# Token halves sharing a PSUM bank, the first 128 tokens alone through the normalisation chain, and the state parts of block 0 last

## The chip, the cores and the metric

The kernel runs on one core of one Trainium2 chip. The metric is the device time of one execution in microseconds (us); the profile's span is about 1.8 us shorter than that time. Before the change the median was 182.52 us over four runs (182.48 to 182.59).

The engines are named as the profile names them: PE (TensorE matmuls), PEld (its weight loads), DVE (VectorE), ACT (ScalarE), POOL (GpSimd), SP (the queue that issues most DMA transfers). PE writes its results to PSUM, in banks that the kernel uses 512 columns at a time; an eviction is the copy of a result out of a bank by DVE or ACT. A transfer lands when its last data has arrived. A hole is a stretch in which PE stands still.

## The reference

A layer normalisation of `x` (2048 tokens, 512 channels) feeds two branches, a diagonal state-space model and a gated feed-forward network. Both are added to `x`:

```python
xn = layernorm(x)
# A: Bu = xn @ B_bar ; h_t = Lam_bar * h_(t-1) + Bu_t ; yA = 2*Re(h @ C^T) + xn*Dskip
# B: yB = (gelu(xn @ w_gate) * (xn @ w_up)) @ w_down        (F = 1376 hidden rows)
out = x + yA + yB
```

## The kernel before

The 2048 tokens are cut into four blocks of 512 tokens; a block has four tiles of 128 tokens. For each block PE does gate and up matmuls (GU: 11 row blocks "ft" of 128 hidden rows), state-input matmuls (BU) and down matmuls (DN). A small scheduler in the kernel orders the instructions of each engine from estimated durations; PE and SP keep program order.

Only block 0 is special. Its tokens must be loaded, normalised and transposed before PE has anything to do, and PE is given warm-up matmuls meanwhile. Its first three row blocks are therefore done in token pieces:

```python
def d_pe(n_list):                       # estimate of matmul time for the scheduler
    return sum(max(n / 2.4 + 2.5, 64.0 + n / 4.7) for n in n_list)

def LN(b, js=range(4), on_act=False):   # statistics, sqrt, reciprocal, scaling of tiles js
    for j in js:
        V(bn_stats ...); V(bn_aggr ...)
    POOL(... mean ...)
    ACT(... variance + eps ...); ACT(... Sqrt ...)      # on_act
    V(reciprocal ...)
    for j in js: V(... (x - mean) * r ...)              # "ln_n"

def GU(b, fts=None, halves=False):
    ...                                 # two banks for each row block: gate, up
    if halves:
        for ft in fts: banks[ft] = (next_bank(), next_bank())
        part(WG, WGc, 0, 0, 1)          # gate, tile 0, three row blocks: 12 matmuls, N=128
        part(WG, WGc, 0, 1, 2)          # gate, tile 1
        part(WU, WUc, 1, 0, 2)          # up, tiles 0 and 1 together: N=256
        TR0(2, "V"); TR0(3, "A")        # transposes of tiles 2, 3; evicted by DVE and by ACT
        part(WG, WGc, 0, 2, 3); part(WG, WGc, 0, 3, 4); part(WU, WUc, 1, 2, 4)
    for ft in fts:
        ...                             # gelu on ACT, copy of up on ACT, product on DVE (512 columns)

# [cut] DN(b): for each tile j: seed, 11 hidden matmuls, 8 state matmuls, add, store

PE(fwarm, ...)                          # 11 warm-up matmuls, N=512
LN(0, [0, 1], True)
TR0(0, "V"); TR0(1, "A"); fill(4); params()
LN(0, [2, 3], True)
load_B()
GU(0, [0, 1, 2], halves=True)
tables_dve()
GU(0, [3, 4])
# [cut] tables, BU(0), CHAIN(0), ..., BU(1), ..., DN(0), ...
```

The loads go to SP in this order: tiles 0 to 3 of x (128 KB each), the first gate chunk (three row blocks, 384 KB), the first up chunk (384 KB), the second gate and the second up chunk (four row blocks, 512 KB each), then block 1's x and the transposing loads of B.

## Time and profile before

| | before |
|---|---|
| median time | 182.52 us |
| span | 180.8 us |
| PE, DVE, ACT busy | 97%, 86%, 51% |
| first gate matmul starts | 6.84 us |
| first state-input matmul of block 0 starts | 16.93 us |
| last matmul ends | 177.75 us |

From the page of the kernel before: busy time of each engine (share of the span, instructions).

```profile
span 180.8 us, 2356 instructions
...
PE 175.2 (97%) x848; PEld 82.8 (46%) x864; DVE 155.8 (86%) x264; ACT 92.0 (51%) x158; POOL 7.5 (4%) x19
```

The same kernel by windows: the head (first gate matmul to first state-input matmul) and the rest up to the last matmul. The columns are the length, each engine's busy time with its instructions, the granted clock, the DMA share and GB/s.

```profile
6.80:16.93 10.13, 9.36 (x97) 7.07 (x97) 9.45 (x29) 7.36 (x14) 2.34 (x3) 1.00 1.15 265
16.93:177.75 160.82, 160.02 (x730) 73.45 (x743) 141.61 (x222) 82.44 (x140) 3.88 (x6) 1.00 0.22 51
```

The second window holds 744 matmuls of 512 columns by the program (some records are missing in the trace). 160.82 us for 744 is 216 ns each. PE is busy through the window, so nothing in it is to be won from waits. What the change can touch is the head. All that PE waited for, by the view of waits (us in total, times, longest):

```profile
PE PS L790 <- DVE arena L508: 1.0, 1, 1.0
PE PS L717 <- DVE arena L637: 0.7, 1, 0.7
```

The head in order of time, PE (start us, duration, line, shapes, count; in brackets the idle time before and what ended it). L790 is the warm-up, L629 the tile transposes, L717 gate and up, L654 state input:

```profile
0.99 4.88 PE L790 MATMUL PS<-arena 128*128 128x512 bf16 x11 [0.99 <-DVE arena L508]
5.80 0.72 PE L629 MATMUL PS<-arena 128*128 128x128 bf16 x8
...
6.84 2.81 PE L717 MATMUL PS<-arena 128*128 128x128 bf16 x36
9.49 0.61 PE L629 MATMUL PS<-arena 128*128 128x128 bf16 x8
10.82 6.28 PE L717 MATMUL PS<-arena 128*128 128x128 bf16 x51 [0.72 <-DVE arena L637]
16.93 7.07 PE L654 MATMUL PS<-arena 128*128 128x512 bf16 x32
```

How to read this: the last number before "x" is the shape of the first matmul of the row only. The bracketed idle time is counted from the modelled end of the matmul before, which includes its drain; from start to start a hole is some 0.16 us longer. The hole at 10.1 to 10.8 us is where PE waits until tiles 2 and 3 have been normalised and evicted.

ACT in the same stretch: tile 3's eviction stands ahead of the load of gelu's table.

```profile
10.13 0.60 ACT L635 ACTIVATE arena<-PS 128x512 bf16<-128x512 bf16 x1 [2.06 <-PE PS L629]
10.75 1.28 ACT L745 ACT_TABLE_LOAD   x1
```

### The profile page before, as it was taken

The numbers are of one execution on the slowest core, as the hardware profiler recorded it, in microseconds if no ns is written. First come the engines' busy times: TensorE is split into PE (matmuls) and PEld (weight loads), VectorE is DVE, ScalarE is ACT, GpSimd is POOL, SyncE is SP. The second block draws the span as 40 slices with busy tenths as digits, with TensorE's granted clock in tenths as the row PEclk, the third lists the DMA queues.
The fourth block names the chain that finished last, engine by engine and source line by source line (L and its number), as shares of the span: only waits on it lengthen the run. The fifth ranks groups of instructions, "written<-read, shape, count | busy, mean of one in ns | idle before, by whom it ended". The sixth has DMA issues, their size and how long they took to land.

```text
span 180.8 us, 2356 instructions
## 1 busy us (share of the span) xinstructions
PE 175.2 (97%) x848; PEld 82.8 (46%) x864; DVE 155.8 (86%) x264; ACT 92.0 (51%) x158; POOL 7.5 (4%) x19
## 2 busy tenths in 40 slices
PE   7989999999999999999999999999999999999993
PEld 2674444444444444444444444444444444444441
DVE  4899679999999996999999999999989999982111
ACT  3378999776767997002667793000667700800000
POOL 2220202000000002000000000000000000000000
PEclk9999999999999999999999999999999999999999
DMA  5999914999000000001610000000000000021100
GB/s 128 305 325 165 313 31 103 244 320 189 14 0 0 4 0 0 29 29 60 90 30 0 0 2 0 33 29 29 29 0 0 4 0 0 0 87 35 54 31 29
DMA packets 24068, 12.38 MB, mean 68 GB/s; under 512 B 15385, under 2 KB 24057, under 8 KB 24057
## 3 DMA queue, kind: packets, MB, share of 16 engines
q1 hardware_dynamic: 24032, 12.23, 28.2%
q8 instruction: 7, 0.11, 0.2%
q14 instruction: 5, 0.03, 0.1%
q10 hardware_dynamic: 24, 0.00, 0.0%
HBM read 6.46 MB, written 2.10 MB: 47 GB/s over the span
## 4 chain that ended last, share of the span: by engine, by line
PE 95%; DVE 2%; issue 1%; ACT 0%; DVEq 0%
PE PS L717 41%; PE PS L773 36%; PE PS L654 15%; PE PS L790 3%; DVE arena L637 0%; DVE arena L608 0%; DVE arena L778 0%; DVE arena L595 0%; PE PS L629 0%; ACT arena L599 0%; ACT arena L600 0%; DVE arena L539 0%; DVE arena L596 0%; DVE arena L538 0%; DVE arena L553 0%
## 5 line engine op out<-in xcount | busy, mean ns | idle before, releaser
L717 PE MATMUL PS<-arena 128*128 128x512 bf16 (+3 forms) x393 | 76.7, 353 | 1.1 <-DVE arena L637 0.7
L773 PE MATMUL PS<-arena 128*128 128x512 bf16 (+1 forms) x296 | 65.6, 379 | 0.4
L717 PEld LDWEIGHTS PS<-arena 128*128 128x128 bf16 (+1 forms) x400 | 37.8, 100 | 38.9 <-DVE arena L637 0.9
L745 ACT ACTIVATE arena<-PS 128x512 bf16<-128x512 f32 (+1 forms) x44 | 26.3, 599 | 49.1 <-PE PS L717 37.1
L773 PEld LDWEIGHTS PS<-arena 128*128 128x128 bf16 (+1 forms) x304 | 29.7, 98 | 36.0
L687 DVE TENSOR_TENSOR_SCAN arena<-arena 128x512 bf16<-128x512 f32 x32 | 38.6, 1251 | 0.0
L748 ACT ACTIVATE arena<-PS 128x512 bf16<-128x512 f32 (+1 forms) x44 | 26.3, 600 | 6.7 <-PE PS L717 6.6
L654 PE MATMUL PS<-arena 128*128 128x512 bf16 x127 | 28.2, 379 | 0.1
L778 DVE TENSOR_TENSOR arena<-PS,arena 128x512 bf16<-128x512 f32 x16 | 10.8, 684 | 15.5 <-PE PS L773 15.5
L654 PEld LDWEIGHTS PS<-arena 128*128 128x128 bf16 x128 | 12.5, 98 | 15.0
L658 ACT ACTIVATE arena<-PS 128x512 bf16<-128x512 f32 x32 | 17.8, 596 | 2.1 <-PE PS L654 2.1
L750 DVE TENSOR_TENSOR arena<-arena 128x512 bf16<-128x512 bf16 (+1 forms) x44 | 17.4, 415 | 0.8 <-ACT arena L748 0.8
L595 DVE BATCH_NORM_STATS2 arena<-arena 128x6 f32<-128x512 bf16 x16 | 10.2, 680 | 3.5 <-DMA arena<-in_A_x_dram 3.5
L760 ACT ACTIVATE PS<-arena 128x512 f32<-128x512 bf16 x16 | 9.4, 603 | 0.7
L674 DVE TENSOR_TENSOR arena<-arena 128x4096 bf16<-128x4096 bf16 (+1 forms) x5 | 9.3, 1859 | 0.0
L676 DVE TENSOR_TENSOR arena<-arena 128x4096 bf16<-128x4096 bf16 (+1 forms) x5 | 9.3, 1858 | 0.0
L699 DVE TENSOR_TENSOR arena<-arena 128x4096 bf16<-128x4096 bf16 x4 | 9.2, 2288 | 0.1
L700 DVE TENSOR_TENSOR arena<-arena 128x4096 bf16<-128x4096 bf16 x4 | 9.1, 2284 | 0.0
L608 DVE TENSOR_SCALAR arena<-arena 128x512 bf16<-128x512 bf16 x16 | 5.6, 409 | 0.3
L615 DVE TENSOR_TENSOR arena<-arena 128x512 bf16<-128x512 bf16 x16 | 5.8, 416 | 0.0
L790 PE MATMUL PS<-arena 128*128 128x512 bf16 x11 | 4.9, 632 | 1.0 <-DVE arena L508 1.0
L571 DVE SCALAR_TENSOR_TENSOR arena<-arena 128x512 bf16<-128x512 bf16 x8 | 5.6, 747 | 0.0
(75 smaller groups left out, 66.1 us busy)
## 6 DMA issues: line engine op xcount, KB each, us to landing
out_dram<-arena SPq DMA_DIRECT2D x16, 128.0 KB, 1.7
arena<-in_A_x_dram SPq DMA_DIRECT2D x3, 512.0 KB, 7.6
arena<-in_B_w_down_dram SPq DMA_DIRECT2D x1, 1280.0 KB, 8.2
arena<-in_A_x_dram SPq DMA_DIRECT2D x4, 128.0 KB, 2.2
arena<-in_B_w_gate_dram SPq DMA_DIRECT2D x1, 512.0 KB, 5.8
arena<-in_B_w_up_dram SPq DMA_DIRECT2D x1, 512.0 KB, 6.7
arena<-in_B_w_gate_dram SPq DMA_DIRECT2D x1, 480.0 KB, 4.6
arena<-in_B_w_up_dram SPq DMA_DIRECT2D x1, 480.0 KB, 6.0
```

Source lines behind the costliest of these rows:

```text
L595: V(lambda e, tt=tt: e.bn_stats(ST[tt].ap, X[tt].ap), d_dve_1x(512), [X[tt]], [ST[tt]], "bnst")
L654: ins_ = e.matmul(PS[bank][:, :], BBT[c][dk].ap[:, 128 * s:128 * (s + 1)], XNT[b].ap[:, dk, :], start=(dk == 0), stop=(dk == KD - 1))
L658: ACT(lambda e, bank=bank, k3=k3, s=s, c=c: e.activation(SSc[k3][s][c].ap, PS[bank][:, :], ACTF.Copy), d_act(512), [BANK[bank]], [SSc[k3][ ...
L687: V(lambda e, g=g, rb=rb, init=init: e.tensor_tensor_scan(g.ap, rb, g.ap, init, ALU.mult, ALU.add), d_dve_scan(512), [g, PA[RRr]] + ([CARc ...
L717: ins_ = e.matmul(PS[bank][0:m, c0:c1], W.ap[:, dk, 128 * ft:128 * ft + m], XNT[b].ap[:, dk, c0:c1], start=(dk == 0), stop=(dk == KD - 1))
L745: GATE["last_gelu"] = ACT(lambda e, bg=bg, kk=kk, m=m: e.activation(GG[kk].ap[0:m, :], PS[bg][0:m, :], ACTF.Gelu_apprx_tanh), d_act(512), ...
L748: ACT(lambda e, bu=bu, kk=kk, m=m: e.activation(UPB[kk].ap[0:m, :], PS[bu][0:m, :], ACTF.Copy), d_act(512), [BANK[bu]], [UPB[kk]], "evU")
L750: V(lambda e, kk=kk, m=m, ft=ft, k2=k2: e.tensor_tensor(HTt[k2][ft].ap[0:m, :], GG[kk].ap[0:m, :], UPB[kk].ap[0:m, :], ALU.mult), d_dve_tt ...
L760: ACT(lambda e, bank=bank, tt=tt: e.activation(PS[bank][:, :], X[tt].ap, ACTF.Copy), d_act(512), [X[tt]], [BANK[bank]], "seed")
L773: ins_ = e.matmul(o_, l_, r_, start=False, stop=(n == len(mms) - 1), skip_group_check=True)
L778: V(lambda e, bank=bank, ko=ko, tt=tt: e.tensor_tensor(OUTB[ko].ap, PS[bank][:, :], XD[tt].ap, ALU.add), d_dve_1x(512), [BANK[bank], XD[tt ...
L790: ins_ = e.matmul(PS[wb][:, :].rearrange("p (a b) -> p a b", a=4), WRM.ap, wrm4, start=True, stop=True)
```

## The change

The intent: get the first tile to PE sooner by not making it wait for the second tile's statistics, and let a row block's gate and up results of half the tokens (256 columns each) share one 512-column bank, so that five row blocks can be worked on in halves. Block 0's down part first takes all hidden matmuls and then the state matmuls, to give block 0's states more time. The scheduler's estimates of matmul time and of the delay between matmuls are corrected.

```diff
+LAT = lambda d, op: SYNC_LAT if d.kind == "dma" or d.eng != op.eng else (0.0 if d.eng == "tensor" else SELF_LAT)
     # [cut] LAT used in the scheduler's two passes in place of SELF_LAT / SYNC_LAT
 def d_pe(n_list):
-    return sum(max(n / 2.4 + 2.5, 64.0 + n / 4.7) for n in n_list)
+    return sum(n / 2.4 + 2.5 for n in n_list)
 # [cut] LN takes "after", added to bn_stats
+        def GU_first(fts, early, single):
+            banks = [{ft: next_bank() for ft in fts} for h in range(2)]
+            def mm(ft, u, j0, j1):      # gate (u=0) in columns 0-255 of the bank, up (u=1) in 256-511
+                ...
+            def evac(ft, h, ...):       # gelu, copy and product of 256 columns
+                ...
+            for u in range(2):
+                for ft in early:
+                    mm(ft, u, 0, 1)                     # tile 0: gate, then up
+                    if single and u == 0 and ft == 1:
+                        TR0(1, "A")
+            for ft in early:
+                for u in range(2):
+                    mm(ft, u, 1, 2)                     # tile 1
+                evac(ft, 0)
+            late = [ft for ft in fts if ft not in early]
+            mm(late[0], 0, 0, 2)
+            TR0(2, "V")
+            TR0(3, "A")
+            for ft in late[1:]:
+                mm(ft, 0, 0, 2)
+            for ft in late:
+                mm(ft, 1, 0, 2)
+                evac(ft, 0)
+            for ft in fts:
+                for u in range(2):
+                    mm(ft, u, 2, 4)                     # second token half
+                evac(ft, 1)
 # [cut] GU loses its halves; DN is split into seed, hidden, states, store
+            if split:
+                for j in range(4):
+                    seed(j); hidden(j)
+                for j in range(4):
+                    states(j); store(j)
-        LN(0, [0, 1], True)
+        LN(0, [0], True)
         TR0(0, "V")
-        TR0(1, "A")
         fill(4)
         params()
-        LN(0, [2, 3], True)
+        LN(0, [1], True, [GATE["bnag"]])
+        LN(0, [2, 3], True, [GATE["evT"]])
         load_B()
-        GU(0, [0, 1, 2], halves=True)
+        GU_first(range(5), range(3), True)
         tables_dve()
-        GU(0, [3, 4])
 # [cut]
-        DN(0)
+        DN(0, True)
```

Gate and up in one bank are safe here because their accumulation groups follow one another and are never open together. The Trainium skill ("PSUM — Partial Sum Buffer", "The four PSUM rules") says that a group's first matmul clears the accumulation bits of the whole bank, and that two open groups cannot both do that.

More of the change, by code (lines that the diff above doesn't have):

```diff
@@ L203, in _backward @@
             for d in op.deps:
-                late[d.id] = min(late[d.id], begin[op.id] - (SELF_LAT if d.eng == op.eng and d.kind == "eng" else SYNC_LAT))
+                late[d.id] = min(late[d.id], begin[op.id] - LAT(d, op))
                 left[d.id] -= 1
@@ L224, in rdy_time @@
         def rdy_time(op):
-            return max([d.finish + (SELF_LAT if d.eng == op.eng and d.kind == "eng" else SYNC_LAT) for d in op.deps], default=0.0)
+            return max([d.finish + LAT(d, op) for d in op.deps], default=0.0)
         while nleft:
@@ L543, in build @@
         W16p = [A.sub(A.alloc("W16v", [4, 4], F32, at=W16.lo), "W16_%d" % i, i) for i in range(4)]
-        GATE = {"before_gelu": []}
+        GATE = {"before_gelu": [], "nh": 0}
         sinT, sinP, cosT, cosP = (SC16.ap[:, 4 * i:4 * i + 4] for i in range(4))
@@ L587, in tables_act, with LN @@
             return ACT(lambda e: e.activation(SINT.ap, F1.ap, ACTF.Sin, scale=-SIN_SCALE), d_act(2048), [F1], [SINT], "sint", after=[t])
-        def LN(b, js=range(4), on_act=False):
+        def LN(b, js=range(4), on_act=False, after=()):
             j0, j1 = js[0], js[-1] + 1
@@ L594, in LN @@
                 tt = 4 * b + j
-                V(lambda e, tt=tt: e.bn_stats(ST[tt].ap, X[tt].ap), d_dve_1x(512), [X[tt]], [ST[tt]], "bnst")
-                V(lambda e, tt=tt, j=j: e.bn_aggr(MVt[b][j].ap, ST[tt].ap), D_TINY, [ST[tt]], [MVt[b][j]], "bnag")
+                V(lambda e, tt=tt: e.bn_stats(ST[tt].ap, X[tt].ap), d_dve_1x(512), [X[tt]], [ST[tt]], "bnst", after)
+                GATE["bnag"] = V(lambda e, tt=tt, j=j: e.bn_aggr(MVt[b][j].ap, ST[tt].ap), D_TINY, [ST[tt]], [MVt[b][j]], "bnag")
             POOL(lambda e: e.tensor_copy(mn.ap, mv.ap[:, :, 0]), 200, [mv], [mn], "mn")
@@ L704, in CHAIN, with f, evac @@
               d_dve_tt2x(2048), [TA, TB], [SSc[k3][s][1] for s in range(KP)], "post_im")
-        def GU(b, fts=None, halves=False):
+        def GU_first(fts, early, single):
+            banks = [{ft: next_bank() for ft in fts} for h in range(2)]
+            def mm(ft, u, j0, j1):
+                W, Wc = ((WG, WGc), (WU, WUc))[u]
+                h, q0 = j0 // 2, 256 * u + 128 * (j0 % 2)
+                bank = banks[h][ft]
+                def f(e):
+                    ins_ = None
+                    for dk in range(KD):
+                        ins_ = e.matmul(PS[bank][:, q0:q0 + 128 * (j1 - j0)], W.ap[:, dk, 128 * ft:128 * (ft + 1)],
+                                        XNT[0].ap[:, dk, 128 * j0:128 * j1], start=(dk == 0), stop=(dk == KD - 1))
+                    return ins_
+                PE(f, d_pe([128 * (j1 - j0)] * 4), [Wc[wchunk(ft)]] + XT0[j0:j1], [BANK[bank]], "GU0")
+            def evac(ft, h):
+                bank, c0 = banks[h][ft], 256 * h
+                GATE["nh"] = kk = (GATE["nh"] + 1) % 3
+                GATE["last_gelu"] = ACT(lambda e: e.activation(GG[kk].ap[:, 0:256], PS[bank][:, 0:256], ACTF.Gelu_apprx_tanh),
+                                        d_act(256), [BANK[bank]], [GG[kk]], "gelu")
+                ACT(lambda e: e.activation(UPB[kk].ap[:, 0:256], PS[bank][:, 256:512], ACTF.Copy),
+                    d_act(256), [BANK[bank]], [UPB[kk]], "evU")
+                V(lambda e: e.tensor_tensor(HTt[0][ft].ap[:, c0:c0 + 256], GG[kk].ap[:, 0:256], UPB[kk].ap[:, 0:256], ALU.mult),
+                  d_dve_tt2x(256), [GG[kk], UPB[kk]], [HTt[0][ft]], "hmul")
+            for u in range(2):
[20 more added lines that the diff above has]
+                evac(ft, 1)
@@ L707, in GU @@
+        def GU(b, fts=None):
             k2 = b % 2
@@ L720, in mm @@
                 PE(f, d_pe([c1 - c0] * 4), [Wc[wchunk(ft)]] + rd, [BANK[bank]], "GU%d" % b)
-            if halves:
-                for ft in fts:
-                    banks[ft] = (next_bank(), next_bank())
-                def part(W, Wc, i, j0, j1):
-                    for ft in fts:
-                        mm(ft, W, Wc, banks[ft][i], 128 * j0, 128 * j1, XT0[j0:j1])
-                part(WG, WGc, 0, 0, 1)
-                part(WG, WGc, 0, 1, 2)
-                part(WU, WUc, 1, 0, 2)
-                TR0(2, "V")
-                TR0(3, "A")
-                part(WG, WGc, 0, 2, 3)
-                part(WG, WGc, 0, 3, 4)
-                part(WU, WUc, 1, 2, 4)
             for ft in fts:
                 m = FROWS[ft]
-                if not halves:
-                    banks[ft] = (next_bank(), next_bank())
+                banks[ft] = (next_bank(), next_bank())
                 bg, bu = banks[ft]
                 kk = (KF * b + ft) % 3
-                if not halves:
-                    for (W, Wc, bank) in zip((WG, WU), (WGc, WUc), banks[ft]):
-                        mm(ft, W, Wc, bank, 0, 512, XTr(b))
+                for (W, Wc, bank) in zip((WG, WU), (WGc, WUc), banks[ft]):
+                    mm(ft, W, Wc, bank, 0, 512, XTr(b))
                 GATE["last_gelu"] = ACT(lambda e, bg=bg, kk=kk, m=m: e.activation(
@@ L752, in GU, with DN @@
                   d_dve_tt2x(512), [GG[kk], UPB[kk]], [HTt[k2][ft]], "hmul")
-        def DN(b):
+        def DN(b, split=False):
             k2, k3 = b % 2, b % 3
-            for j in range(4):
-                tt = 4 * b + j
-                bank = next_bank()
-                ko = tt % 4
-                ACT(lambda e, bank=bank, tt=tt: e.activation(PS[bank][:, :], X[tt].ap, ACTF.Copy),
-                    d_act(512), [X[tt]], [BANK[bank]], "seed")
-                def f(e, bank=bank, j=j, k2=k2, k3=k3, b=b):
-                    mms = []
-                    for ft in range(KF):
-                        m = FROWS[ft]
-                        mms.append((PS[bank][:, :], HTt[k2][ft].ap[0:m, 128 * j:128 * (j + 1)], WD.ap[0:m, ft, :]))
-                    for s in range(KP):
-                        for c in range(2):
-                            mms.append((PS[bank][:, :], SSc[k3][s][c].ap[:, 128 * j:128 * (j + 1)], CT[c][s].ap))
-                    ins_ = None
-                    for n, (o_, l_, r_) in enumerate(mms):
-                        ins_ = e.matmul(o_, l_, r_, start=False, stop=(n == len(mms) - 1), skip_group_check=True)
-                    return ins_
-                rds = [HTt[k2][ft] for ft in range(KF)] + WDc
-                rds += [SSs[k3][s] for s in range(KP)] + [CT[c][s] for c in range(2) for s in range(KP)]
-                PE(f, d_pe([512] * (KF + 8)), rds + [BANK[bank]], [BANK[bank]], "DN%d" % b)
-                V(lambda e, bank=bank, ko=ko, tt=tt: e.tensor_tensor(OUTB[ko].ap, PS[bank][:, :], XD[tt].ap, ALU.add),
@@ new lines, in DN, with seed, mms, f @@
+            banks = [next_bank() for _ in range(4)]
+            def seed(j):
+                tt, bank = 4 * b + j, banks[j]
+                ACT(lambda e: e.activation(PS[bank][:, :], X[tt].ap, ACTF.Copy), d_act(512), [X[tt]], [BANK[bank]], "seed")
+            def mms(j, ops, last, rds):
+                bank = banks[j]
+                def f(e):
+                    ins_ = None
+                    for n, (l_, r_) in enumerate(ops):
+                        ins_ = e.matmul(PS[bank][:, :], l_[:, 128 * j:128 * (j + 1)], r_, start=False,
+                                        stop=last and n == len(ops) - 1, skip_group_check=True)
+                    return ins_
+                PE(f, d_pe([512] * len(ops)), rds + [BANK[bank]], [BANK[bank]], "DN%d" % b)
@@ new lines, in hidden, with states, store @@
+            def hidden(j):
+                ops = [(HTt[k2][ft].ap[0:FROWS[ft], :], WD.ap[0:FROWS[ft], ft, :]) for ft in range(KF)]
+                mms(j, ops, False, [HTt[k2][ft] for ft in range(KF)] + WDc)
+            def states(j):
+                ops = [(SSc[k3][s][c].ap, CT[c][s].ap) for s in range(KP) for c in range(2)]
+                mms(j, ops, True, [SSs[k3][s] for s in range(KP)] + [CT[c][s] for c in range(2) for s in range(KP)])
+            def store(j):
+                tt, bank = 4 * b + j, banks[j]
+                ko = tt % 4
+                V(lambda e: e.tensor_tensor(OUTB[ko].ap, PS[bank][:, :], XD[tt].ap, ALU.add),
@@ L779, in DN @@
                   d_dve_1x(512), [BANK[bank], XD[tt]], [OUTB[ko]], "evO")
-                S.dma(lambda e, tt=tt, ko=ko: e.dma_start(out[0, 128 * tt:128 * (tt + 1), :], OUTB[ko].ap),
+                S.dma(lambda e: e.dma_start(out[0, 128 * tt:128 * (tt + 1), :], OUTB[ko].ap),
                       128 * 1024, reads=[OUTB[ko]], is_output=True, tag="st_out")
+            if split:
[3 more added lines that the diff above has]
+                    states(j); store(j)
+            else:
+                for j in range(4):
+                    seed(j); hidden(j); states(j); store(j)
```

## The prediction

> **What bounds the kernel now.** TensorE. The page shows PE busy 97% of 180.8 us; the chain of waits is 95% PE. From 16.93 us, where the timeline shows block 0's first state-input matmul, to the last matmul's end at 177.75, there are 744 matmuls of 512 columns at 216 ns: 160.7 us, the whole stretch. Nothing to win there: PE's waits are 1.0 us at the start and 0.7 at 10.8. The change can pay only before 16.93.
>
> **The head before (timeline).** Eleven warm-up matmuls hold the in-order PE from 0.99 to 5.87. Tile 0's ln_n is ready at 5.7, its transposes run at 5.80, its DVE eviction 6.27-6.69, the first gate matmul at 6.84. Then come 48 matmuls of 128 columns, 24 of 256 and 16 of 512, with one hole of 0.72 us before 10.82. Spacing read there: about 56, 109 and 216 ns, as the Trainium skill's "TensorE: Matmul & The Clock Gate", section "Back-to-back issue gap", gives for isolated warm matmuls (N/2.4+2.5); its 81 ns for N=128 is not seen here.
>
> **What the change does.**
> - Tile 0's bn_stats no longer waits for tile 1's (0.69 us), so ln_n ends at about 5.0. But the warm-up is unchanged and blocks PE to about 5.7, and the first weight chunk lands at 2.65+4.0 = 6.65. First gate matmul at about 6.68: only 0.15 us earlier.
> - PE work in fts 0-4: 48x56 + 56x109 = 8.8 us, against 8.76: equal.
> - ACT: 20 evictions of 256 columns (estimate 0.39 us each, 0.27 apart, from 0.60 and 0.48 at 512) for 10 of 512: 0.6 us more, off the chain.
> - PE reaches the second token half (needs tiles 2 and 3) at about 12.05. Tile 3's eviction now stands on ACT behind the 1.28 us gelu table load (possible only after the last sqrt, about 9.4) and four half evictions; before, it stood ahead. Estimate: load ends 10.7, eviction 11.8-12.4. Tile 2's stands on DVE behind an hmul that waits for those evictions: ends about 12.1. PE waits about 0.4 us. The skill's "ScalarE: Activation LUTs", "What ACT_TABLE_LOAD costs", gives 1283 ns, as this trace does; its further drain of about 1380 ns is not seen here.
> - The second half: 40x109 = 4.4 us, ending at 16.86 against 16.93.
> - Block 0's state parts last: its states are ready at 60.1, its down matmuls start at 67.17, so nothing waited. Worth 0.
>
> **Predicted time.** 0.1 to 0.3 us gained: 182.3 us, range 181.5 to 183.2 (8 in 10). Faster by over 2%: 0.01; within 2%: 0.98; slower by over 2%: 0.01.
>
> **What would show it.** First gate matmul at 6.6-6.75. A PE wait of 0.2-0.8 us at about 12, ended by the eviction of tile 2 or 3, in place of the 0.72 us hole. First state-input matmul within 0.7 us of 16.9. From there 160.7 us without a PE wait. DVE busy up by about 0.7 us.
>
> **What would make it wrong.** Weight chunks (landing about 7.73, 9.5, 10.9) are needed within 0.3 us of landing; a late one stalls PE. If tiles 2 and 3 are evicted before 12.05, PE runs unbroken and the gain is 0.7 us. If DVE's order drags tile 1 (its reciprocal now stands behind tile 0's eviction), stalls at 7.2 and 8.4 could add up to 0.5 us of loss. A changed order on DVE or ACT could open a wait in the long stretch, where the slack is 5 to 7 us.

## The result, and the profile after

The median after the change is 182.37 us over four runs (181.93 to 182.48), against 182.52 us. A ratio here is the mean time of one kernel's fast runs over that of the other's in the same rounds, so it is not quite the ratio of the medians. This one is 0.9987, with a 95% interval of 0.9970 to 1.0004: no difference clear of noise. In a later set of five rounds the same kernel gave 0.9982 (0.9970 to 0.9994), a gain of about 0.3 us. The profiled run after the change, at 182.48 us, is the slowest of its four.

The page of the changed kernel:

```profile
span 180.7 us, 2411 instructions
...
PE 174.4 (97%) x865; PEld 84.2 (47%) x880; DVE 156.7 (87%) x270; ACT 93.9 (52%) x170; POOL 9.7 (5%) x20
```

Its windows, the head and the rest:

```profile
6.60:16.85 10.25, 9.65 (x116) 8.85 (x117) 8.54 (x30) 8.39 (x23) 1.26 (x2) 1.00 1.12 269
16.85:177.67 160.82, 160.02 (x731) 73.43 (x743) 144.16 (x229) 83.06 (x142) 6.99 (x7) 1.00 0.21 52
```

The long stretch is 160.82 us again. The last matmul ends at 177.67 and not at 177.75, so the profiled run shows 0.08 us of gain, all of it in the head. PE's waits:

```profile
PE PS L839 <- DVE arena L509: 1.0, 1, 1.0
PE PS L718 <- DVE arena L609: 0.7, 1, 0.7
PE PS L718 <- DMA arena<-in_B_w_up_dram: 0.6, 1, 0.6
PE PS L630 <- DVE arena L609: 0.2, 1, 0.2
```

The head in order of time, PE (L839 warm-up, L630 transposes, L718 gate and up of block 0's first five row blocks, L655 state input; the record of the first state-input matmul is missing, its weight load ran at 16.74, and the second started at 17.06, so one spacing of 0.216 us earlier puts its start at 16.85):

```profile
0.99 4.03 PE L839 MATMUL PS<-arena 128*128 128x512 bf16 x11 [0.99 <-DVE arena L509]
5.19 0.40 PE L630 MATMUL PS<-arena 128*128 128x128 bf16 x4 [0.16 <-DVE arena L609]
...
6.63 0.62 PE L718 MATMUL PS<-arena 128*128 128x128 bf16 x8 [0.71 <-DVE arena L609]
7.08 0.39 PE L630 MATMUL PS<-arena 128*128 128x128 bf16 x4
7.31 0.39 PE L718 MATMUL PS<-arena 128*128 128x128 bf16 x4
8.27 2.62 PE L718 MATMUL PS<-arena 128*128 128x128 bf16 x40 [0.57 <-DMA arena<-in_B_w_up_dram]
10.72 0.61 PE L630 MATMUL PS<-arena 128*128 128x128 bf16 x8
11.17 5.84 PE L718 MATMUL PS<-arena 128*128 128x256 bf16 x52
```

The hole has moved. It is no longer at 10.1 us, but at 7.5 us: PE has done tile 0's gate matmuls and now wants the first up chunk, which before was wanted only after 24 gate matmuls. The chunk was issued at 3.13 us and landed 5.1 us later, at 8.22 us. From the list of DMA issues (KB each, us from issue to landing):

```profile
arena<-in_B_w_gate_dram SPq DMA_DIRECT2D x1, 384.0 KB, 3.9
arena<-in_B_w_up_dram SPq DMA_DIRECT2D x1, 384.0 KB, 5.1
```

The first gate matmul, at 6.63, follows a landing too: the first gate chunk was issued at 2.66 and landed at 6.56, while tile 0's eviction had ended at 6.04 us. The view of waits puts that wait down to DVE; the weight-load row before the same matmul names the gate chunk:

```profile
6.62 0.45 PEld L718 LDWEIGHTS PS<-arena 128*128 128x128 bf16 x8 [0.80 <-DMA arena<-in_B_w_gate_dram]
```

ACT in the same stretch (L601 is the last square root, L726 and L728 are half evictions, the first of four shown, L636 is tile 3's eviction):

```profile
8.41 0.20 ACT L601 ACTIVATE arena<-arena 128x2 bf16<-128x2 bf16 x1
8.63 1.28 ACT L726 ACT_TABLE_LOAD   x1
...
9.93 0.38 ACT L726 ACTIVATE arena<-PS 128x256 bf16<-128x256 f32 x1
...
11.37 0.60 ACT L636 ACTIVATE arena<-PS 128x512 bf16<-128x512 bf16 x1 [0.23 <-PE PS L630]
```

The load and four half evictions do stand ahead of tile 3's eviction, as predicted, but in this run PE is late anyway and nothing comes of it.

### The profile page after: what moved, and what is told of

Same layout as the page of the kernel before. It is cut to its first block, busy times and chain, and to the rows that moved or that the text cites. A ratio compares the mean times of both kernels' runs of the same rounds, so it can differ in the third digit from the quotient of the medians.

```text
span 180.7 us, 2411 instructions
## 1 busy us (share of the span) xinstructions
PE 174.4 (97%) x865; PEld 84.2 (47%) x880; DVE 156.7 (87%) x270; ACT 93.9 (52%) x170; POOL 9.7 (5%) x20
## 3 DMA queue, kind: packets, MB, share of 16 engines
HBM read 6.46 MB, written 2.10 MB: 47 GB/s over the span
## 4 chain that ended last, share of the span: by engine, by line
PE 93%; DMA 3%; SPq 1%; issue 1%; DVE 0%; DVEq 0%
PE PS L767 37%; PE PS L802 36%; PE PS L655 15%; PE PS L718 5%; DMA arena<-in_B_w_up_dram 3%; SPq L465 1%; DVE arena L818 0%; PE PS L630 0%; SPq L461 0%; DVEq L331 0%
## 5 line engine op out<-in xcount | busy, mean ns | idle before, releaser
L767 PE MATMUL PS<-arena 128*128 128x512 bf16 (+1 forms) x308 | 67.8, 379 | 0.2
L802 PE MATMUL PS<-arena 128*128 128x512 bf16 (+1 forms) x297 | 65.8, 379 | 0.4
L767 PEld LDWEIGHTS PS<-arena 128*128 128x128 bf16 (+1 forms) x312 | 31.4, 100 | 36.1
L779 ACT ACTIVATE arena<-PS 128x512 bf16<-128x512 f32 (+1 forms) x39 | 23.5, 603 | 46.2 <-PE PS L767 36.8
L802 PEld LDWEIGHTS PS<-arena 128*128 128x128 bf16 (+1 forms) x304 | 29.7, 98 | 36.0
L655 PE MATMUL PS<-arena 128*128 128x512 bf16 x124 | 27.7, 379 | 0.2
L782 ACT ACTIVATE arena<-PS 128x512 bf16<-128x512 f32 (+1 forms) x39 | 23.5, 602 | 7.2 <-PE PS L767 7.1
L655 PEld LDWEIGHTS PS<-arena 128*128 128x128 bf16 x128 | 12.5, 98 | 14.8
L784 DVE TENSOR_TENSOR arena<-arena 128x512 bf16<-128x512 bf16 (+1 forms) x39 | 15.5, 414 | 3.6 <-ACT arena L782 3.3
L596 DVE BATCH_NORM_STATS2 arena<-arena 128x6 f32<-128x512 bf16 x16 | 10.3, 682 | 1.4 <-DMA arena<-in_A_x_dram 1.3
L718 PE MATMUL PS<-arena 128*128 128x256 bf16 (+1 forms) x104 | 9.5, 248 | 1.3 <-DVE arena L609 0.7
L718 PEld LDWEIGHTS PS<-arena 128*128 128x128 bf16 x104 | 8.1, 98 | 2.1 <-DMA arena<-in_B_w_gate_dram 0.8
```

The costliest lines, as they stand in the source:

```text
L596: V(lambda e, tt=tt: e.bn_stats(ST[tt].ap, X[tt].ap), d_dve_1x(512), [X[tt]], [ST[tt]], "bnst", after)
L655: ins_ = e.matmul(PS[bank][:, :], BBT[c][dk].ap[:, 128 * s:128 * (s + 1)], XNT[b].ap[:, dk, :], start=(dk == 0), stop=(dk == KD - 1))
L718: ins_ = e.matmul(PS[bank][:, q0:q0 + 128 * (j1 - j0)], W.ap[:, dk, 128 * ft:128 * (ft + 1)], XNT[0].ap[:, dk, 128 * j0:128 * j1], start=( ...
L767: ins_ = e.matmul(PS[bank][0:m, c0:c1], W.ap[:, dk, 128 * ft:128 * ft + m], XNT[b].ap[:, dk, c0:c1], start=(dk == 0), stop=(dk == KD - 1))
L779: GATE["last_gelu"] = ACT(lambda e, bg=bg, kk=kk, m=m: e.activation(GG[kk].ap[0:m, :], PS[bg][0:m, :], ACTF.Gelu_apprx_tanh), d_act(512), ...
L782: ACT(lambda e, bu=bu, kk=kk, m=m: e.activation(UPB[kk].ap[0:m, :], PS[bu][0:m, :], ACTF.Copy), d_act(512), [BANK[bu]], [UPB[kk]], "evU")
```

## The experiments

Twelve runs were made, the changed kernel once more and eleven variants, all with correct results. They ran in four groups, each on one chip with its own runs of the kernel before: after_again to before_w_first; no_split to evict_first; old_model, gate_first and gate_first_x1_late; weights_last alone. Only one run of each is profiled, and it can be the fastest or the slowest. A useful constant: in all of them the time from the first state-input matmul of block 0 to the end of the last matmul was 160.81 to 160.82 us. So the start of that first matmul, given below for each, says where the profiled run's head stands (16.93 before, 16.85 after). A second constant is the head without any wait: 48 matmuls at 56 ns, 56 at 109 ns and 8 transposes at 56 ns are 9.24 us, and 9.46 us where tile 1's transposes fall into it too. (For gate_first, gate_first_x1_late and weights_last it is 24 at 56 ns, 68 at 109 ns and 8 transposes: 9.20 us.)

**First theory:** the changed head is bound by the landing of the first up chunk. **Rival:** it is bound by the chain on DVE and ACT (tile 1's eviction ends at 8.11 us, just as late), or the gain comes from the shorter chain and something else takes it away.

### after_again: the changed kernel, unaltered

> The changed kernel, unaltered, so that the other runs have it on their own chip. Theory (the up-weight landing binds the head): 182.0 to 182.5 us; PE's wait for the first up-weight chunk is there again (0.3 to 0.9 us, ended by that landing at 7.9 to 8.4 us), and where the landing is earlier by some amount, the whole run is shorter by the same. Rival (the head is bound by DVE and ACT: tile 1's eviction, ending at 8.11): the run does not follow the landing.

Measured: 182.35 us (181.99 to 182.46), before 182.59; ratio 0.9982 (0.9970 to 0.9994). The wait for the up chunk did **not** return. In this run the chunk landed at 7.2 us, and there is the other hole, the predicted one:

```profile
6.78 0.61 PE L718 MATMUL PS<-arena 128*128 128x128 bf16 x8 [0.28 <-DVE arena L605]
...
7.51 2.83 PE L718 MATMUL PS<-arena 128*128 128x128 bf16 x44
10.18 0.61 PE L630 MATMUL PS<-arena 128*128 128x128 bf16 x8
10.63 1.47 PE L718 MATMUL PS<-arena 128*128 128x256 bf16 x12
12.36 4.53 PE L718 MATMUL PS<-arena 128*128 128x256 bf16 x40 [0.26 <-DVE arena L537]
```

ACT in the same run:

```profile
9.22 1.28 ACT L726 ACT_TABLE_LOAD   x1
...
11.59 0.63 ACT L636 ACTIVATE arena<-PS 128x512 bf16<-128x512 bf16 x1
```

The twelve matmuls from 10.63 take 12 x 109 ns, to 11.94. PE goes on at 12.36, so the hole is 0.42 us from start to start, 0.14 us after tile 3's eviction ended at 12.22. (The row names a tiny DVE instruction that ended last; tile 3's eviction is what these matmuls read, and evict_first and old_model below bear that out.) First state-input matmul at 16.73. So a single cause does not hold: the changed head has two holes, one for the up chunk and one for tile 3, and the later PE comes out of the first, the less it finds of the second.

### w_first: the first weight chunks ahead of tiles 2 and 3 of x

```diff
-        for j in range(4):
+        for j in range(2):
             ld_x0(j)
         ld_w(WG, ..., 0); ld_w(WU, ..., 0)
+        for j in range(2, 4):
+            ld_x0(j)
```

> The changed kernel, with the first gate and up chunks queued ahead of the x tiles 2 and 3 (about 0.9 us earlier). Theory: first gate matmul at about 6.15 in place of 6.63 (then tile 0's eviction ends last), up chunk lands at about 7.2, PE's wait for it is gone or under 0.2 us, block 0's first state-input matmul at about 16.2 in place of 16.85; 0.5 to 0.9 us faster than the changed kernel, so about 181.6. A new wait of 0.3 to 0.5 us for tile 3's eviction at about 11.5 is then likely. Rival (DVE and ACT bind): less than 0.15 us gained, PE waits at 7.5 to 8.2 for tile 1's eviction instead.

Measured: 182.46 us; ratio 0.9993 (0.9981 to 1.0005). The up chunk landed at 6.9 us and the wait for it is gone, as expected, but the first state-input matmul came at 16.79 and not at 16.2. The first gate matmul came at 6.72 us, not at 6.15, because the warm-up matmuls ran at the slow rate (427 ns apart) to the end and the transposes started only at 5.65. The second gate chunk, which landed at about 9.8, held PE for some 0.2 us. And the last 52 matmuls took 6.21 us where they take 5.84 unbroken: the hole for tile 3's eviction is there, 0.37 us, as the expectation had called likely.

The later load of tiles 2 and 3 is not what opens that hole. The later of the two landed at 7.18 us, and their statistics began at 7.20 (6.55 after the change); but in after_again, with the loads in their old place, they began at 7.14, since there too the warm-up ended late. The first row is of after_again, the others are of w_first:

```profile
7.14 1.28 DVE L596 BATCH_NORM_STATS2 arena<-arena 128x6 f32<-128x512 bf16 x2
7.20 1.29 DVE L598 BATCH_NORM_STATS2 arena<-arena 128x6 f32<-128x512 bf16 x2
10.75 6.21 PE L720 MATMUL PS<-arena 128*128 128x256 bf16 x52
```

So w_first repeats after_again: with the up chunk on time, PE meets the second hole.

### up_late: the first up chunk behind the second gate chunk

```diff
         ld_w(WG, ..., 0)
-        ld_w(WU, ..., 0)
         ld_w(WG, ..., 1)
+        ld_w(WU, ..., 0)
```

> The changed kernel, with the first up chunk queued behind the second gate chunk: the suspected wait made longer on purpose. Theory: the up chunk lands at about 9.4, PE's wait grows from 0.6 to about 1.8 us, block 0's first state-input matmul moves from 16.85 to about 18.0, the time rises by 1.0 to 1.3 us. Rival: the time rises by under 0.5 us.

Measured: 183.86 us; ratio 1.0093 (1.0056 to 1.0131). PE waited 1.4 us for the up chunk (landing at about 9.7), the first state-input matmul came at 18.31, 1.46 us later. A late up chunk costs what it is late. One of the four runs, 185.88 us at clock 0.991, widens the interval; the others lie between 183.69 and 183.93. (This profiled run also started its gate matmuls at 7.21, 0.6 us late, since the gate chunk took 4.5 us.)

### before_w_first: the kernel before, with the early weight chunks

The same edit as w_first, on the kernel before.

> The kernel before, with the same early queueing of the first weight chunks. Theory: nothing gained (under 0.15 us), since there tile 0's eviction at 6.69 ends last and the up chunk is wanted only after 36 gate matmuls; the 0.72 us hole at 10.1 to 10.8 stays. Rival (earlier weights help whatever the order of work): 0.5 us or more gained.

(The up chunk is wanted there after 24 gate matmuls, not 36; the 36 in PE's row are 24 gate and 12 up matmuls.)

Measured: 183.01 us; ratio 1.0024 (1.0011 to 1.0036). No gain, as the theory had it, but it overlooked the price: DVE waited 0.54 us for the later x tiles (both statistics began at 7.23 us; the kernel before had done tile 2's at 4.28 and began tile 3's, the last, at 6.61), PE had to wait 0.43 us to transpose them, and the first state-input matmul came at 17.61. What the weight chunks gained, the x tiles lost: their median from issue to landing rose from 2.2 to 3.2 us, in w_first as here.

### no_split: block 0's down part as before

```diff
-        DN(0, True)
+        DN(0)
```

> The changed kernel with the down part of block 0 as before (hidden and state matmuls of each 128 tokens together). Theory: worth nothing; within 0.15 us of the changed kernel (182.2 to 182.5), PE shows no wait where the down part of block 0 begins, at about 67.1 us. Rival (the split gives the slack that the changed order needs): PE waits for the states at 67 to 72 us and the time is 0.3 us or more longer.

Measured: 182.36 us; ratio 0.9980 (0.9967 to 0.9994), the same as the changed kernel's 0.9982 (on another chip). No PE wait from 66.9 us on; its long stretch is 160.82 us. The split is worth nothing here. This profile also shows a third hole that one landing can open: the second gate chunk came at about 10.3 us, and PE, done with the 40 matmuls before at about 9.4 (7.20 + 40 x 56 ns), stood still until then. First state-input matmul at 17.02. (This is the slowest of its six runs, 182.65 us.)

```profile
10.36 0.61 PE L718 MATMUL PS<-arena 128*128 128x256 bf16 x4 [0.76 <-DMA arena<-in_B_w_gate_dram]
```

### banks_only: tiles 0 and 1 together through the chain, bank sharing kept

```diff
-        LN(0, [0], True)
-        TR0(0, "V"); fill(4); params()
-        LN(0, [1], True, [GATE["bnag"]])
-        LN(0, [2, 3], True, [GATE["evT"]])
+        LN(0, [0, 1], True)
+        TR0(0, "V"); TR0(1, "A"); fill(4); params()
+        LN(0, [2, 3], True)
-        GU_first(range(5), range(3), True)
+        GU_first(range(5), range(3), False)
```

> The changed kernel with tiles 0 and 1 again together through the normalisation chain; bank sharing and the down order kept. Theory (the single-tile chain buys nothing, because the warm-up and the first weight chunks hold PE; tile 1 comes later for it): first gate matmul at about 6.85; no wait for tile 1; PE waits only for the first up chunk, if that lands after 7.5. Block 0's first state-input matmul between 16.1 (chunk lands by 7.5) and 16.9 (chunk lands at 8.2); not slower than the changed kernel: 181.7 to 182.5. Rival (the short chain is where the gain comes from): as slow as before, 182.5 to 182.7, or slower.

Measured: 182.18 us; ratio 0.9974 (0.9960 to 0.9987). Without the single-tile chain the kernel is no slower. First gate matmul at 6.98, a wait for the up chunk (landing at 8.0), first state-input matmul at 16.69, no hole at 12 us: the square roots of tiles 2 and 3 come sooner, so the table load starts at 8.24.

### chain_only: the single-tile chain on the kernel before

```diff
-        LN(0, [0, 1], True)
-        TR0(0, "V"); TR0(1, "A"); fill(4); params()
-        LN(0, [2, 3], True)
+        LN(0, [0], True)
+        TR0(0, "V"); fill(4); params()
+        LN(0, [1], True, [GATE["bnag"]])
+        LN(0, [2, 3], True, [GATE["evT"]])
 ...
                 part(WG, WGc, 0, 0, 1)
+                TR0(1, "A")
```

> The kernel before with the first tile alone through the chain; two banks for each row block and the old matmul order kept. Theory: PE runs out of work on tile 0 (12 gate matmuls) at about 7.5 and waits about 0.7 us for tile 1's eviction, which ends near 8.4; block 0's first state-input matmul at 17.2 to 17.5; 0.2 to 0.5 us slower than before, about 182.9. Rival (the short chain is where the gain comes from): 0.15 us or more faster than before.

Measured: 183.14 us; ratio 1.0025 (1.0012 to 1.0038), slower than before. The waits of this profile:

```profile
PE PS L717 <- ACT arena L635: 0.7, 1, 0.7
PE PS L717 <- DVE arena L637: 0.6, 1, 0.6
```

PE ran out of work on tile 0 and waited for tile 1's eviction until 8.63 us; then for tile 2's until 11.86. First state-input matmul at 17.97, later than the 17.2 to 17.5 expected: the second wait, the hole of the kernel before a microsecond later, had not been expected. (The profiled run, 183.60 us, is the slowest of the five.) The short chain alone is a loss, and in the changed kernel it is not where a gain comes from.

### evict_first: tile 3's eviction ahead of the gelu table load

The half evictions of the first three row blocks come in the program after `TR0(3, "A")`, and their gelus depend on both evictions:

```diff
             for ft in early:
                 for u in range(2):
                     mm(ft, u, 1, 2)
-                evac(ft, 0)
 ...
             TR0(3, "A")
+            for ft in early:
+                evac(ft, 0, [GATE["evT"], GATE["evT3"]])
```

> The changed kernel, with the gelu evictions of the first three row blocks held back until tiles 2 and 3 are evicted, so that tile 3's eviction stands on ACT before the gelu table load again. Theory (the prediction's step: the load and four evictions ahead of it make PE wait at about 12): no PE wait at 12; block 0's first state-input matmul at about 16.5 where the up chunk lands by 7.6, and unchanged at about 16.85 where it lands at 8.2; on the mean 0.1 to 0.3 us faster than the changed kernel. Rival (late gelus hold banks and buffers): a new PE wait at 12 to 17 us, and no gain or a loss.

Measured: 182.08 us; ratio 0.9970 (0.9956 to 0.9985), against 0.9980 for no_split of the same rounds, which is the changed kernel but for a part worth nothing. ACT now evicts tile 3 at 11.23 and loads the table after it:

```profile
11.23 0.60 ACT L636 ACTIVATE arena<-PS 128x512 bf16<-128x512 bf16 x1 [0.50 <-PE PS L630]
11.90 1.28 ACT L726 ACT_TABLE_LOAD   x1
```

There is no hole at 12 us: tile 3's eviction ended at 11.83, and PE wanted it at 12.34 (11.03 + 12 x 109 ns). But the up chunk came at 8.1 in this run, which held PE by some 0.3 us and by itself makes that hole smaller; the first state-input matmul is at 16.70. The later gelus opened no new wait. The gain of about 0.2 us is of the size expected, but the two intervals overlap, so it is not shown clear of noise.

### old_model: the scheduler's estimates as before

```diff
 def d_pe(n_list):
-    return sum(n / 2.4 + 2.5 for n in n_list)
+    return sum(max(n / 2.4 + 2.5, 64.0 + n / 4.7) for n in n_list)
     # and LAT as in the kernel before
```

> The changed kernel, with the estimates of the scheduler (matmul times, and the delay between matmuls) as before; this moves only the order of instructions on DVE and ACT. Theory: the long stretch stays full (160.7 us); in the head tile 3's eviction stands behind six half evictions on ACT in place of four, so PE waits 0.5 to 0.9 us at about 12 where the up chunk lands early, and 0 to 0.4 us more than the changed kernel in the mean: 182.4 to 182.8. Rival (the estimates are where the gain comes from): as slow as before or slower, 182.6 or more, with waits in the long stretch.

Measured: 183.04 us, before 182.73; ratio 1.0011 (0.9995 to 1.0026). This is worse than expected: with the old estimates the change is no gain at all. The instructions are the same; ACT takes six half evictions ahead of tile 3's, which then ends at 12.88, and not at 11.97 or 12.22 as in the two profiles of the changed kernel:

```profile
12.22 0.66 ACT L636 ACTIVATE arena<-PS 128x512 bf16<-128x512 bf16 x1
```

PE waits for it, and here the row names it:

```profile
10.75 1.47 PE L718 MATMUL PS<-arena 128*128 128x256 bf16 x12
13.03 4.53 PE L718 MATMUL PS<-arena 128*128 128x256 bf16 x40 [0.81 <-ACT arena L636]
```

First state-input matmul at 17.39. The rival had said waits in the long stretch; there are none (160.82 us). So what the corrected estimates buy shows in ACT's order, two half evictions fewer (2 x 0.26 us) ahead of the one that PE waits for; by the ratios, from different rounds on the same chip, it is about 0.5 us (the intervals just miss each other, at 0.9994 and 0.9995).

### gate_first: banks_only, and gate matmuls of both tiles before any up matmul

```diff
-            for u in range(2):
-                for ft in early:
-                    mm(ft, u, 0, 1)
-            for ft in early:
-                for u in range(2):
-                    mm(ft, u, 1, 2)
-                evac(ft, 0)
+            for j in range(2):
+                for ft in early:
+                    mm(ft, 0, j, j + 1)
+            for ft in early:
+                mm(ft, 1, 0, 2)
+                evac(ft, 0)
```

> Bank sharing with tiles 0 and 1 together through the chain (as banks_only), and PE takes the gate matmuls of both tiles first, the up matmuls (256 columns) of both after: the first up chunk is wanted 0.67 us later, at about 8.2. Theory (the order in which weights are wanted against their landings): no wait for the first up chunk, or under 0.1 us; block 0's first state-input matmul at about 16.1 if the second gate chunk lands by 9.6, later by its lateness if not (it landed between 9.1 and 10.3 so far); 181.6 to 182.1 us. Rival (PE is held by the chain of evictions, not by landings): same as banks_only, within 0.1 us of 182.2, with a wait for DVE or ACT in its place.

Measured: 182.00 us (181.71 to 182.07), before 182.73; ratio 0.9957 (0.9945 to 0.9969). This is the fastest of all kernels by the ratio, and clear of noise against the kernel before, but its interval overlaps those of banks_only, evict_first, gate_first_x1_late and weights_last. (One run of the kernel before in these rounds took 1063 us; it counts as slow and is left out of the ratio.) The head as a window, and PE's rows:

```profile
6.87:16.09 9.22, 9.22 (x101) 8.43 (x101) 8.10 (x29) 8.07 (x23) 1.26 (x2) 1.00 1.11 270
```

```profile
6.87 3.26 PE L718 MATMUL PS<-arena 128*128 128x128 bf16 x40
9.96 0.61 PE L630 MATMUL PS<-arena 128*128 128x128 bf16 x8
10.41 5.84 PE L718 MATMUL PS<-arena 128*128 128x256 bf16 x52
16.09 2.11 PE L655 MATMUL PS<-arena 128*128 128x512 bf16 x9
```

PE is busy 9.22 of 9.22 us in the head. The first up chunk landed at 7.9 us, so late that the order of banks_only, which wants it at about 7.5, would have waited for it; here it was wanted at 8.2 us. The first state-input matmul came at 16.09, as expected, 0.60 us before that of banks_only: 0.46 of it is the wait for the up chunk there (7.65 to 8.11), 0.11 an earlier first gate matmul. That is a comparison of two profiled runs, and gate_first's is the fastest of its five. By the ratios, from different chips, the gain over banks_only is about 0.3 us, with intervals that overlap.

### gate_first_x1_late: block 1's x queued later

```diff
         def load_B():
-            ld_x(1)
             load_T(B_re)
+            ld_x(1)
             load_T(B_im)
```

> As gate_first, with the 512 KB of block 1's x queued behind the transposing load of B's real part, so at about 12 us and not at 4.8. Theory: the second gate and up chunks share the DMA engines with less and land 0.3 to 1.0 us earlier (gate by 9.2, up by 10.4); no PE wait for a landing; block 0's first state-input matmul at 16.0 to 16.2; the fastest kernel so far, 181.4 to 181.8. Rival (DMA is not what sets the head): no change against gate_first. Danger: block 1's x lands late for the statistics of block 1 at about 17 us, or B's parts land late for 16.1 us.

Measured: 182.17 us (181.66 to 182.45); ratio 0.9969 (0.9955 to 0.9983). It failed: not faster than gate_first, and the second chunks landed 5.6 and 6.5 us after issue, exactly as in gate_first's profile. The profiled run, the fastest of the six, has a nearly full head (first state-input matmul at 16.05), but others of its runs are slower. They have no profile, so what held them isn't known; queueing block 1's x later did not remove it.

### weights_last: every chunk wanted later than it can be late

On gate_first: the transposes of tiles 2 and 3 come before the second gate chunk is wanted, the second token half of the first three row blocks comes before the second up chunk is wanted, and the evictions are ordered as in evict_first.

```diff
             for ft in early:
                 mm(ft, 1, 0, 2)
-                evac(ft, 0)
-            mm(late[0], 0, 0, 2)
             TR0(2, "V"); TR0(3, "A")
-            for ft in late[1:]:
+            for ft in early:
+                evac(ft, 0, [GATE["evT"], GATE["evT3"]])
+            for ft in late:
                 mm(ft, 0, 0, 2)
+            for ft in early:
+                for u in range(2):
+                    mm(ft, u, 2, 4)
+                evac(ft, 1)
             for ft in late:
                 mm(ft, 1, 0, 2)
                 evac(ft, 0)
-            for ft in fts:
+            for ft in late:
                 ...
```

> As gate_first, and two things more. PE turns to the transposes of tiles 2 and 3 before the second gate chunk is wanted, and takes the second token half of the first three row blocks before it wants the second up chunk (wanted at about 13.5 in place of 10.85); the gelu evictions of the first three row blocks come after tiles 2 and 3, as in evict_first. Theory (in the runs of gate_first that are slower than its profiled one, a weight chunk lands late): no PE wait after the first gate matmul; block 0's first state-input matmul at 16.0 to 16.2 in every run, so 181.6 to 181.8 us with a spread under 0.2 us. Rival (what varies from run to run is something else, such as when the clock is released or later waits): the spread of 0.3 us or more stays, median 181.9 or more. Danger: the gelus come 2.5 us later and ACT falls behind, so PE waits for a bank at 14 to 18 us.

Measured: 182.05 us (182.03 to 182.19); ratio 0.9970 (0.9957 to 0.9984). Half of the theory held. The spread of the five runs is 0.16 us, less than half of that of gate_first (on another chip), and PE did not wait after the first gate matmul. But the level is not 181.7: the first gate matmul came at 7.03 us, 0.16 later than in gate_first's profiled run, and the first state-input matmul at 16.30. More of the transposes ran at the slow rate (107 ns apart in place of 56), so the eight took 0.82 us and not 0.72, and tile 0's eviction began at 6.46 and not at 6.22. So gate_first remains the best by ratio, and its slower runs are as slow as these.

The traces show one thing that varies at the start: when PE changes from the slow rate to the fast. Five profiles have the changed kernel's start. Where the rate changed before the transposes (no_split: four transposes in 0.39 us), the first gate matmul came at 6.47 us; where the transposes and the filler still ran slowly (evict_first: 0.63 us each), at 6.90. How much of the difference from run to run this makes, beside the landings, stays open.

## Why the prediction was right or wrong

The time was right: 182.3 predicted, 182.37 measured.

- **"The change can pay only before 16.93": right.** The long stretch is 160.82 us before, after and in all twelve experiments. That the block's state parts last are "worth 0" is shown by no_split (0.9980 against 0.9982).
- **"First gate matmul at about 6.68: only 0.15 us earlier": right.** It came at 6.63 and 6.78 in the two profiles of the changed kernel, in one held by the gate chunk (landing at 6.56; the warm-up blocked PE there to 5.0 only, not to 5.7), in the other by the late end of the warm-up (transposes at 5.66). In the three other profiles with this start it came at 6.47 to 6.90, so the band of 6.6 to 6.75 is narrower than the spread. The shortened chain (0.69 us of bn_stats) ends in front of those two. chain_only and banks_only show that this part of the change brings nothing or harm.
- **PE work "equal" (8.8 us against 8.76): right.** In the profile PE ran unbroken from 8.27 to 16.85, 8.58 us; its 36 matmuls at 56 ns, 56 at 109 ns and eight transposes at 56 ns make 8.57. The head of gate_first is 9.22 us, by the same sum for its order 9.20.
- **"PE waits about 0.4 us" at 12 us, for tile 3's eviction behind the table load: right in mechanism and size, but not in every run.** It was 0.42 us in the second profile (after_again) and 0.37 in w_first, absent in the profile on record, 0.97 us from start to start with six evictions ahead (old_model, 12.06 to 13.03), and gone where the eviction comes first (evict_first, where a late up chunk helped).
- **Where it was wrong:** "Weight chunks (landing about 7.73, 9.5, 10.9) are needed within 0.3 us of landing" stood only among the risks, with landings taken from a single profile. The first up chunk landed anywhere from 7.2 to 8.2 us in the profiles with this order of loads, the second gate chunk from 9.2 to 10.3 (issue times plus times to landing, in the lists of DMA issues). In the profile on record this cost 0.74 us (7.53 to 8.27) in place of the predicted hole. The mis-sized term is that landing. The total came out right because the two holes stand in for one another: whichever comes first delays PE past the second. That the prediction's figure for the first state-input matmul, 16.86, met the measured 16.85 is therefore partly luck.
- **Left out:** the corrected estimates of the scheduler were only mentioned as a risk. old_model shows that without them the change would have been no gain (1.0011).
- **A small term off:** ACT was to rise by 0.6 us; its busy time rose by 1.9 (92.0 to 93.9). The 0.6 counted the spacing of evictions (0.27 us), the busy time counts their length (20 x 0.39 against 10 x 0.60), and the extra square-root pair adds 0.5; evictions that overlap (0.27 apart, 0.39 long) bring the sum of 2.3 down. It is off the chain. DVE rose by 0.9, predicted 0.7.

Where did the expected gain go? Of the 0.7 us hole that the change set out to fill and the 0.69 us cut from the chain, nearly all was lost to waits that had been hidden behind them: the warm-up and the first gate chunk in front, then the first up chunk, which the new order wants 0.7 us sooner, or tile 3's eviction behind a table load.

## What to carry to other kernels

When an engine is full from some point on, a change ahead of that point is worth at most the holes there, and those holes stand in a row: cutting one shows the next. List for each piece of early work when it is wanted and when its inputs land, over several profiles and not one, and order the work so that each transfer is wanted later than its latest landing; here that gave the best ratio (gate_first, 0.9957), while the shorter chain gave nothing. And see where a one-time table load falls in an engine's queue: what stands behind it can be late by its whole length, 1.28 us here.

## What the Trainium skill lacked or had wrong

- "TensorE: Matmul & The Clock Gate", "Back-to-back issue gap": it gives about 81 ns per matmul of 128 columns in a real stream of weight load and matmul, and about 131 ns for 512 columns, and calls N/2.4 + 2.5 ns the isolated gap. Here every matmul has its own weight load, and the stream runs at the isolated figure: 216 ns at 512 columns (160.82 us for 744) and about 56 and 109 ns at 128 and 256 (24 at 128, 68 at 256 and eight transposes make 9.20 us; the whole head of gate_first took 9.22).
- "ScalarE: Activation LUTs", "What ACT_TABLE_LOAD costs": the 1283 ns are confirmed (1283 ns in each of these profiles), but not the further drain of about 1380 ns for every switch: in the changed kernel the square root before it ended at 8.61, the load ran from 8.63 to 9.91 and the first gelu started at 9.93.
- "TensorE: Matmul & The Clock Gate", "Part 1: The HAM clock gate": it says that the window is free-running and that the point at which matmuls become fast therefore varies by 500 ns either way. It varied by more here. The warm-up always starts at 0.99 us; in the changed kernel's profile its matmuls go from 427 to 217 ns apart about 3.1 us after the first, and in old_model matmuls of 128 columns are still 107 ns apart at 6.08 us, 5.1 us after the first (four took 0.64 us there, against 0.39). The same eleven warm-up matmuls took 4.03, 4.16, 4.30, 4.65 and (most often) 4.87 us.
- No page was found to give the spread of a transfer's landing from run to run. The same 384 KB in the same place of the same queue, issued at 3.13 us, took from 4.1 to 5.1 us here.
